# Sparse attention and a feed-forward layer on one core: decoding the weights by a parametric Relu, and batch 1 in two rounds of visits

## The chip, the cores and the metric

The kernel runs on one core of a Trainium2 chip. The core has TensorE (matrix products into PSUM; PE in the profile, PEld its weight loads), VectorE (DVE), ScalarE (ACT), GpSimd (POOL) and the DMA queues that SyncE (SP) starts. The metric is the device time of one execution in microseconds; lower is better.

## The reference, cut to what matters

Eight batches, eight heads, 576 tokens, 64 columns per head. Scores below the row's maximum less tau are dropped; the attention output of all heads is one row of 512 per token and goes through a feed-forward layer with weights of 512 x 2048 and 2048 x 512.

```python
scores = scale * np.matmul(q, k.transpose(0, 1, 3, 2))
thresh = np.max(scores, axis=-1, keepdims=True) - tau
scores = np.where(scores >= thresh, scores, -1000000000.0)
scores = scores - np.max(scores, axis=-1, keepdims=True)
attn = np.exp(scores)
attn = attn / (np.sum(attn, axis=-1, keepdims=True) + 1e-09)
attn_out = np.matmul(attn, v)
...
h = x @ w_in
g = h * (1.0 / (1.0 + np.exp(-h)))
return (g @ w_out).astype(np.float32)
```

q, k and v are float32; the weights are float64, and the kernel is handed their raw 64-bit words.

## The kernel before, in words

**Order of the work.** One Python loop runs over score tiles; a list `todo` hangs other steps on tile numbers. A tile is 128 query rows of one head against 576 keys (or 64 rows of two heads). `visits` lists pairs of heads: batch 0 is visited in two rounds, "low" (the first 256 query columns, four tiles a pair) and "high" (the other 320, five tiles), and every later batch in one ("all", nine tiles, query columns in two ranges of 288). The loop holds 12 empty steps between the rounds of batch 0 (tiles 16 to 27) and one ahead of batch 1, whose tiles are 49 to 84; batch 2 begins at 85. A scheduler orders the instructions of each engine at compile time from the order in which they are emitted, priorities (`pri`) and a model of their times; each engine then runs its list in order.

**A tile.** Two products of the query tile with the rounded keys and their remainder (L412); VectorE finds the maximum (L422); ScalarE takes exponentials (L432); VectorE masks and sums (L441); ScalarE normalises (L454). GpSimd makes two halves of 16 bits of the result (L465, L468, L471; for tiles below 36 ScalarE makes the first, L463). A DMA transpose brings them into `wT`, and AV (L496) multiplies them with the halves of V. The low round of batch 0 goes another way (`soft3_direct`, `av_direct`), without halves.

**Keys and queries.** `load_qk` loads K and Q of a head five tiles ahead, each twice (two halves of the partitions). `split_k` rounds K on ScalarE (L324) and takes the remainder on GpSimd (L326). `split_q` does the like for Q; for batch 1 and later on ScalarE (L315) and VectorE (L316).

**Weights.** Each of 32 tiles of 128 x 512 (16 of w_in, 16 of w_out) is loaded as pairs of 32-bit words. `decode_weights`: GpSimd scales the upper word, read as a float, by 2^-112 (L179); VectorE shifts it left by 3, which drops the sign (L183), and ORs in the lower word's top bits (L186); TensorE sums the magnitudes over the partitions with a matrix of ones, four matmuls a tile (L197), which bounds the maximum in every partition (L202); ScalarE takes the sign of the upper word (L204) and GpSimd multiplies by it (L205). Once all 16 tiles of a matrix are decoded, `pow2_scales` makes a power-of-two scale, and `split_weights` makes two 16-bit parts: ScalarE the first (L211), VectorE the second, the scaled weight less the first part (L212). `W_PLAN` hangs decoding of w_in on tiles 0 to 9 and its split on 10 to 12, decoding of w_out on tiles 9 to 21 and its split on 22 to 25.

**Feed-forward units.** When all heads of a column range are through AV, `moe_units` makes units: 16 h units (12 matmuls each, L539, then L547 to L555 on ScalarE and VectorE) and 16 o units (12 matmuls, L570). For batch 0 a range brings both kinds at once. From batch 1 on the o units of a range are held and paired with the h units of the next. The loop issues units by a credit that grows by `rate` a tile: 1.3 and 0.8 for the ranges of batch 0, then the units that are waiting, divided by the tiles until the next batch's range, times 0.95.

Of the kernel before, what the change touches and what calls it, by code (L numbers as in the profile page):

```python
# [40 lines left out]
PRI_AV = 1500  # L41

# [10 lines left out]
def attention_moe(  # L53
# [52 lines left out]
    def pow2_scales(mx, name, across=True):  # L106


        k = name[0]
        one = const.tile([P, 1], F32, name=f"{name}_one", tag=f"{k}_one")  # L110
        nc.vector.tensor_reduce(out=one, in_=mx, op=ALU.max, axis=AX.X)
        if across:


            diag = const.tile([P, P], BF16, name=f"{name}_diag", tag="diag")
            nc.scalar.activation(diag, ident, AF.Copy, scale=one)
            allp = bank([P, P], f"{name}_ps", 0 if turn[1] == 3 else None)
            nc.tensor.matmul(allp, ones, diag, start=True, stop=True)
            one = const.tile([P, 1], F32, name=f"{name}_all", tag=f"{k}_all")
            nc.vector.tensor_reduce(out=one, in_=allp, op=ALU.max, axis=AX.X)  # L120
        cl = const.tile([P, 1], F32, name=f"{name}_cl", tag=f"{k}_cl")
        nc.vector.tensor_scalar(
            out=cl, in0=one, scalar1=2.0**-20, scalar2=2.0**47, op0=ALU.max, op1=ALU.min
        )
        e2 = const.tile([P, 2], I32, name=f"{name}_e2", tag=f"{k}_e2")
        nc.vector.tensor_scalar(
            out=e2[:, 0:1], in0=cl.bitcast(I32), scalar1=EXPMASK, scalar2=None, op0=ALU.bitwise_and
        )
        nc.vector.tensor_scalar(
            out=e2[:, 1:2], in0=cl.bitcast(I32), scalar1=EXPMASK, scalar2=EXPMASK,  # L130
            op0=ALU.bitwise_and, op1=ALU.bitwise_xor,
        )
# [39 lines left out]
    def decode_weights(i):  # L172
# [6 lines left out]
        nc.gpsimd.tensor_scalar(  # L179
            out=w, in0=top.bitcast(F32), scalar1=2.0**-112, scalar2=1.0,  # L180
            op0=ALU.mult, op1=ALU.mult,
# [14 lines left out]
        for j in range(4):  # L196
            nc.tensor.matmul(  # L197
                wps[n], ones, upper[:, j * P : (j + 1) * P],
                start=(c == 0 and j == 0), stop=(c == 3 and j == 3),
            )  # L200
        if c == 3:
            nc.vector.tensor_reduce(out=wmx[:, n : n + 1], in_=wps[n], op=ALU.max, axis=AX.X)  # L202
        sg = stage.tile([P, 512], F16, tag="wsg", name=f"wsg_{i}", bufs=2)
        nc.scalar.activation(sg, top.bitcast(F32), AF.Sign)  # L204
        nc.gpsimd.tensor_tensor(out=w, in0=w, in1=sg, op=ALU.mult)  # L205

    def split_weights(i):
        w = wst[:, i + WSPARE, :]
        hi = w16[:, i, 0:512]
        sc = wsc["in" if i < 4 * NK else "out"][:, 0:1]  # L210
        nc.scalar.activation(hi, w, AF.Copy, scale=sc)  # L211
        nc.vector.scalar_tensor_tensor(  # L212
            out=w16[:, i, 512:1024], in0=w, scalar=sc, in1=hi, op0=ALU.mult, op1=ALU.subtract
        )
# [33 lines left out]
    def vscale(b):  # L248
        vsc[b] = pow2_scales(vmx[b], f"v{b}")
        if b == 0:  # L250
            nc.vector.tensor_scalar(
                out=xscale, in0=vsc[0][:, 0:1], scalar1=2.0**-12, scalar2=None, op0=ALU.mult
            )
# [32 lines left out]
    def load_qk(v, h):  # L286
        b, hh = divmod(h, H)
        qr = sb.tile([P, S], F32, tag="qraw", name=f"qraw_{v}_{h}", bufs=2)
        kr = sb.tile([P, S], F32, tag="kraw", name=f"kraw_{v}_{h}", bufs=2)
        for r in range(2):  # L290
            nc.sync.dma_start(out=kr[r * D : (r + 1) * D, :], in_=kT[b, hh])
            nc.sync.dma_start(out=qr[r * D : (r + 1) * D, :], in_=qT[b, hh])
        qkraw[h] = qr, kr
# [6 lines left out]
    def split_q(h, tiles):  # L300
        qr = qkraw[h][0]
        odd = h % 2
        c0, c1 = 0, S
        if len(tiles) < 4:
            c0, c1 = (0, 320) if odd else (256, S)
# [293 lines left out]
    def moe_units(b, c0, n):  # L599
        if b == 0:  # L600
            return h_units(b, c0, n) + o_units(b, c0, n)
# [11 lines left out]
    visits += [(b, p, "all") for b in range(1, B) for p in range(NPAIR)]  # L613
# [7 lines left out]
    for v, (b, p, kind) in enumerate(visits):  # L621
        if kind == "high" and p == 0:
            tiles.extend([None] * GAP)
            first_high = len(tiles)
        if b == 1 and p == 0:
            tiles.extend([None] * GAP1)
# [14 lines left out]
        if kind == "low":  # L641
# [7 lines left out]
        for h, use, tl, last in ((ha, u, ta, last_a), (ha + 1, use_b, tb + [4] * (4 in ta), last_b)):  # L649
            at(use - LOAD, lambda v=v, h=h: load_qk(v, h))  # L650
# [8 lines left out]
    for b in range(B):  # L659
        u = start[b, 0]  # L660
        for p in range(NPAIR):
# [4 lines left out]
            else:  # L666
                at(u + 9 * p - 40, lambda b=b, p=p: load_v(b, p))
                at(u + 9 * p - 34, lambda b=b, p=p: vmax(b, p))
                at(u + 9 * p + 4, lambda b=b, p=p: split_v(b, p))
# [11 lines left out]
    def scale_in():  # L681
        wsc["in"] = pow2_scales(wmx[:, 0:4], "i_w", across=False)

    def scale_out():
        wsc["out"] = pow2_scales(wmx[:, 4:8], "o_w", across=False)
# [129 lines left out]
```

## Time and profile before

| | us |
|---|---|
| three runs | 1252.15, 1245.27, 1250.52 |
| median | 1250.52 |
| the profiled execution | 1244.94 |
| its span, first to last instruction | 1243.2 |

One execution was profiled. Busy time is what an engine's instructions take; matmuls are pipelined and their ends are modelled, so a busy TensorE is not TensorE at its peak. PEclk is the granted share of TensorE's clock. A group's mean is over all instructions of one line and shape in the stretch that was asked for. What ended an idle time is inferred from semaphores.

### The profile page before, as it was taken

Reading aid. Unit: us, or ns where it says so; the run is one execution under the profiler, and the core shown is the slowest. Engines: PE = TensorE matmul, PEld = TensorE weight load, DVE = VectorE, ACT = ScalarE, POOL = GpSimd, SP = SyncE. Lnnn points to the kernel's source line nnn. Section 1 sums busy time; section 2 is a strip of 40 time slices with the busy share of each in tenths; the row PEclk is TensorE's granted clock in tenths of the full one; section 3 lists DMA queues with packets and bytes.
Section 4 is the critical chain, followed back from the end, with each engine's and each line's share of the span. In section 5 each row is a group of like instructions: output and inputs, shape, how many; then the busy total and the mean of one; then the engine's idle time right before and its main releaser. Section 6 shows DMA issues by size and latency. Waiting matters only on the chain.

```text
span 1243.2 us, 26997 instructions
## 1 busy us (share of the span) xinstructions
PE 1140.7 (92%) x9400; PEld 897.4 (72%) x9400; DVE 961.3 (77%) x2627; ACT 818.0 (66%) x1505; POOL 759.4 (61%) x952
## 2 busy tenths in 40 slices
PE   5674879899799989999999999999999999999998
PEld 3453657676577767777888877787777877777777
DVE  7999998978888888989888957988689848333230
ACT  5787777766777667777777747776577847433331
POOL 4568988577778768786878708773688538200000
PEclk8996889899899999999999999999999999999999
DMA  9457867678868868888778638783687436200000
GB/s 297 127 177 179 186 130 146 132 151 167 151 130 145 166 133 147 148 158 172 143 140 152 137 90 154 143 148 101 110 168 148 87 73 116 54 15 16 12 14 24
DMA packets 363480, 158.15 MB, mean 127 GB/s; under 512 B 329552, under 2 KB 338256, under 8 KB 363344
## 3 DMA queue, kind: packets, MB, share of 16 engines
q1 hardware_dynamic: 363344, 156.43, 61.9%
q8 instruction: 74, 1.21, 0.4%
q14 instruction: 62, 0.51, 0.1%
HBM read 66.72 MB, written 9.44 MB: 61 GB/s over the span
## 4 chain that ended last, share of the span: by engine, by line
PE 54%; DVE 25%; DMA 6%; ACT 6%; issue 5%; POOL 4%; SPq 0%; ACTq 0%; POOLq 0%; DVEq 0%
PE o L570 20%; PE h L539 19%; PE s L412 7%; PE a L496 7%; DVE w L441 6%; DVE sm L422 5%; DMA vraw<-in_vL 3%; DVE qstack L316 3%; ACT w L432 2%; DMA wT<-hl 2%; DVE wst L212 2%; DVE h L548 1%; DVE gbuf L555 1%; ACT w L454 1%; DVE wst L186 1%
## 5 line engine op out<-in xcount | busy, mean ns | idle before, releaser
L539 PE MATMUL h<-x,wst 128*128 128x288 f16 (+2 forms) x3072 | 430.8, 290 | 12.7 <-DVE gbuf L555 10.2
L570 PE MATMUL o<-gbuf,wst 128*128 128x288 f16 (+2 forms) x3072 | 420.6, 287 | 8.2 <-ACT wst L580 6.5
L539 PEld LDWEIGHTS <-wst 128*128 128x128 f16 x3072 | 294.6, 99 | 102.0 <-issue 22.0
L570 PEld LDWEIGHTS <-wst 128*128 128x128 f16 x3072 | 293.2, 98 | 90.5 <-issue 11.4
L468 POOL TENSOR_TENSOR hl<-w,hl 128x512 f16<-128x512 f32 x272 | 329.3, 1211 | 14.5 <-ACT hl L463 2.1
L465 POOL TENSOR_SCALAR hl<-w 128x576 f16<-128x576 f32 x264 | 180.6, 687 | 190.8 <-ACT w L454 128.3
L432 ACT ACTIVATE w<-s,sm 128x576 f32<-128x576 f32 x288 | 210.5, 738 | 83.5 <-DVE sm L422 30.6
L441 DVE SCALAR_TENSOR_TENSOR w<-s,sm,w 128x576 f32<-128x576 f32 x288 | 232.0, 812 | 32.5 <-ACT w L432 30.2
L454 ACT ACTIVATE w<-w,sm 128x576 f32<-128x576 f32 x288 | 217.6, 770 | 52.4 <-DVE sm L449 49.3
L422 DVE TENSOR_REDUCE sm<-s 128x1 f32<-128x576 f32 x288 | 215.0, 749 | 31.9 <-PE s L412 28.2
L548 DVE SCALAR_TENSOR_TENSOR h<-th,h 128x288 f32<-128x288 f32 (+2 forms) x256 | 116.2, 455 | 108.5 <-ACT th L547 106.4
L547 ACT ACTIVATE th<-h,msc 128x288 f32<-128x288 f32 (+2 forms) x256 | 126.2, 497 | 106.0 <-PE h L539 104.7
L412 PE MATMUL s<-khi,qstack 128*128 128x288 f32 x608 | 158.7, 343 | 19.0 <-DVE w L441 14.5
L554 ACT ACTIVATE gbuf<-h 128x288 f16<-128x288 f32 (+2 forms) x256 | 103.5, 407 | 81.3 <-DVE h L548 80.2
L555 DVE SCALAR_TENSOR_TENSOR gbuf<-h,gbuf 128x288 f16<-128x288 f32 (+2 forms) x256 | 114.9, 451 | 40.4 <-ACT gbuf L554 39.6
L496 PE MATMUL a<-wT,v 128*64 128x288 f16 (+1 forms) x1680 | 131.3, 298 | 13.5 <-DMA wT<-hl 13.3
L412 PE MATMUL s<-klo,qstack 128*128 128x288 f32 x608 | 132.6, 300 | 0.0
L326 POOL TENSOR_TENSOR klo<-kraw,khi 128x576 fp32r<-128x576 f32 x64 | 95.2, 1487 | 56.5 <-ACT khi L324 53.8
L412 PEld LDWEIGHTS s<-khi,qstack 128*128 128x128 f32 x608 | 97.9, 196 | 41.9 <-issue 22.9
L496 PEld LDWEIGHTS <-v 128*64 128x64 f16 x1680 | 94.5, 113 | 40.1 <-issue 30.3
L412 PEld LDWEIGHTS s<-klo,qstack 128*128 128x128 f32 x608 | 100.3, 194 | 0.3
L471 POOL TENSOR_TENSOR hl<-w,hl 128x64 f16<-128x64 f32 x272 | 100.2, 368 | 0.0
(84 smaller groups left out, 866.5 us busy)
## 6 DMA issues: line engine op xcount, KB each, us to landing
qraw<-in_qT SPq DMA_DIRECT2D x128, 144.0 KB, 3.0
kraw<-in_kT SPq DMA_DIRECT2D x128, 144.0 KB, 3.0
vraw<-in_vL SPq DMA_DIRECT2D x32, 320.0 KB, 3.7
wraw<-in_w_out SPq DMA_DIRECT2D x16, 512.0 KB, 3.8
out_t<-wst SPq DMA_DIRECT2D x56, 144.0 KB, 2.2
wT<-hl SPq DMA_TRANSPOSE x304, 3.4
gbuf<-in_w_in SPq DMA_DIRECT2D x8, 512.0 KB, 7.5
wraw<-in_w_in SPq DMA_DIRECT2D x8, 512.0 KB, 6.0
```

Of the source, the lines that this page charges most:

```text
L412: nc.tensor.matmul(s_ps[:, j, :HALF], lhs, kk[:, j * HALF : (j + 1) * HALF], start=(n == 0), stop=(n == len(seq) - 1),)
L422: nc.vector.tensor_reduce(out=negm, in_=s_ps[:, :, :HALF], op=ALU.max, axis=AX.XY, negate=True)
L432: nc.scalar.activation(wtile[t].rearrange("p (j c) -> p j c", j=2), sps[t][:, :, :HALF], AF.Exp, bias=small[t][:, 0:1],)
L441: nc.vector.scalar_tensor_tensor(out=w3, in0=s_ps[:, :, :HALF], scalar=sm[:, 1:2], in1=w3, op0=ALU.is_ge, op1=ALU.mult, accum_out=sm[:, 2:3],)
L454: nc.scalar.activation(w, w, AF.Copy, scale=r)
L465: nc.gpsimd.tensor_scalar(out=fl[:, 0:S], in0=w, scalar1=1.0, scalar2=1.0, op0=ALU.mult, op1=ALU.mult)
L468: nc.gpsimd.tensor_tensor(out=fl[:, 640:1152], in0=w[:, 0:512], in1=fl[:, 0:512], op=ALU.subtract)
L496: nc.tensor.matmul(a_ps[odd * D : (odd + 1) * D, :n], vt[:, lo_v, odd, kv, :], wT[v, b * H + 2 * p + odd][:, kw, c0 - base : c0 - base + n ...
L539: nc.tensor.matmul(ph[:, :n], wi(c, f, lo_w), x16[b, lo_x][:, c, c0 : c0 + n], start=(k == 0), stop=(k == 11),)
L548: nc.vector.scalar_tensor_tensor(out=ph[:, :n], in0=th[:, :n], scalar=1.0, in1=ph[:, :n], op0=ALU.add, op1=ALU.mult,)
L555: nc.vector.scalar_tensor_tensor(out=g[:, 1, :n], in0=ph[:, :n], scalar=2.0**-14, in1=g[:, 0, :n], op0=ALU.mult, op1=ALU.subtract,)
L570: nc.tensor.matmul(ps[:, :n], wo(f, d, lo_w), g[:, lo_g, :n], start=(f == 0 and k == 0), stop=(f == NF - 1 and k == 2),)
```

## The change

Weights: ScalarE's Prelu takes the place of GpSimd's scaling. A positive word is scaled by 2^-112, a negative one by 2^-112 times 2^32, so that the bit that the shift by 3 moves into the sign place is set; Sign and the multiplication by it go. As the weights now carry their sign, each part is multiplied with itself, so that the sums of squares stand on the diagonal; `pow2_scales` spreads the maximum over the partitions for the weights too, and halves the exponent of a sum of squares. In the split, GpSimd scales the weight in place, ScalarE casts the first part, and GpSimd takes the difference.

Batch 1: it is visited like batch 0, four low visits and then four high ones, all by the DMA-transposed way. Each head's keys are loaded and split in both rounds, its queries by column ranges. Its first range makes h and o units at once; the second (320 columns) is held and paired with batch 2. The V steps of batch 1 get other tile numbers, and the bank of its V scale is fixed.

```diff
+HALVED = (1,)
...
-    def pow2_scales(mx, name, across=True):
+    def pow2_scales(mx, name, own=None, squared=False):
...
         nc.vector.tensor_reduce(out=one, in_=mx, op=ALU.max, axis=AX.X)
-        if across:
...
+        diag = const.tile([P, P], BF16, name=f"{name}_diag", tag="diag")
+        nc.scalar.activation(diag, ident, AF.Copy, scale=one)
+        allp = bank([P, P], f"{name}_ps", own)
+        nc.tensor.matmul(allp, ones, diag, start=True, stop=True)
+        one = const.tile([P, 1], F32, name=f"{name}_all", tag=f"{k}_all")
+        nc.vector.tensor_reduce(out=one, in_=allp, op=ALU.max, axis=AX.X)
         cl = const.tile([P, 1], F32, name=f"{name}_cl", tag=f"{k}_cl")
+        low, high = (2.0**-40, 2.0**94) if squared else (2.0**-20, 2.0**47)
...
+        if squared:
+            twice = const.tile([P, 1], F32, name=f"{name}_twice", tag=f"{k}_twice")
+            nc.vector.tensor_scalar(
+                out=twice, in0=cl, scalar1=2.0, scalar2=None, op0=ALU.mult
+            )
+            half = const.tile([P, 1], I32, name=f"{name}_half", tag=f"{k}_half")
+            nc.vector.tensor_scalar(
+                out=half, in0=twice.bitcast(I32), scalar1=1, scalar2=EXPMASK,
+                op0=ALU.logical_shift_right, op1=ALU.bitwise_and,
+            )
+            cl = const.tile([P, 1], F32, name=f"{name}_root", tag=f"{k}_root")
+            nc.vector.tensor_scalar(
+                out=cl, in0=half.bitcast(F32), scalar1=2.0**64, scalar2=None, op0=ALU.mult
+            )
...
-        nc.gpsimd.tensor_scalar(
-            out=w, in0=top.bitcast(F32), scalar1=2.0**-112, scalar2=1.0,
-            op0=ALU.mult, op1=ALU.mult,
+        nc.scalar.activation(
+            w, top.bitcast(F32), AF.Prelu, scale=2.0**-112, alpha=2.0**32
         )
...
+            part = upper[:, j * P : (j + 1) * P]
             nc.tensor.matmul(
-                wps[n], ones, upper[:, j * P : (j + 1) * P],
+                wps[n], part, part,
                 start=(c == 0 and j == 0), stop=(c == 3 and j == 3),
             )
...
-        sg = stage.tile([P, 512], F16, tag="wsg", name=f"wsg_{i}", bufs=2)
-        nc.scalar.activation(sg, top.bitcast(F32), AF.Sign)
-        nc.gpsimd.tensor_tensor(out=w, in0=w, in1=sg, op=ALU.mult)
...
-        nc.scalar.activation(hi, w, AF.Copy, scale=sc)
-        nc.vector.scalar_tensor_tensor(
-            out=w16[:, i, 512:1024], in0=w, scalar=sc, in1=hi, op0=ALU.mult, op1=ALU.subtract
+        nc.gpsimd.tensor_scalar(
+            out=w, in0=w, scalar1=sc, scalar2=1.0, op0=ALU.mult, op1=ALU.mult
+        )
+        nc.scalar.activation(hi, w, AF.Copy)
+        nc.gpsimd.tensor_tensor(
+            out=w16[:, i, 512:1024], in0=w, in1=hi, op=ALU.subtract
         )
...
-        vsc[b] = pow2_scales(vmx[b], f"v{b}")
+        vsc[b] = pow2_scales(vmx[b], f"v{b}", (None, 2)[b] if b < 2 else 0)
...
+    def qcols(h, tiles):
+        if len(tiles) > 3:
+            return 0, S
+        if 0 in tiles:
+            return (320, S) if h % 2 else (0, 256)
+        return (0, 320) if h % 2 else (256, S)
+
-    def load_qk(v, h):
+    def load_qk(v, h, tiles):
         b, hh = divmod(h, H)
+        c0, c1 = qcols(h, tiles)
...
             nc.sync.dma_start(out=kr[r * D : (r + 1) * D, :], in_=kT[b, hh])
-            nc.sync.dma_start(out=qr[r * D : (r + 1) * D, :], in_=qT[b, hh])
+            nc.sync.dma_start(out=qr[r * D : (r + 1) * D, c0:c1], in_=qT[b, hh, :, c0:c1])
...
-        if b == 0:
+        if b == 0 or (b == 1 and c0 == 0 and 1 in HALVED):
             return h_units(b, c0, n) + o_units(b, c0, n)
...
-    visits += [(b, p, "all") for b in range(1, B) for p in range(NPAIR)]
+    for b in range(1, B):
+        for kind in ("low", "high") if b in HALVED else ("all",):
+            visits += [(b, p, kind) for p in range(NPAIR)]
...
-                at(u + 9 * p - 40, lambda b=b, p=p: load_v(b, p))
-                at(u + 9 * p - 34, lambda b=b, p=p: vmax(b, p))
-                at(u + 9 * p + 4, lambda b=b, p=p: split_v(b, p))
+                pace, first = (4, 24) if b in HALVED else (9, 40)
+                at(u + pace * p - first, lambda b=b, p=p: load_v(b, p))
+                at(u + pace * p - first + 6, lambda b=b, p=p: vmax(b, p))
+                at(u + pace * p + pace // 2, lambda b=b, p=p: split_v(b, p))
...
-        wsc["in"] = pow2_scales(wmx[:, 0:4], "i_w", across=False)
+        wsc["in"] = pow2_scales(wmx[:, 0:4], "i_w", squared=True)
...
-        wsc["out"] = pow2_scales(wmx[:, 4:8], "o_w", across=False)
+        wsc["out"] = pow2_scales(wmx[:, 4:8], "o_w", 2, squared=True)
```

## Rows read from the trace of the kernel before

**Rows 1.** The page: busy us per engine, and busy tenths in 40 slices.
```profile
PE 1140.7 (92%) x9400; PEld 897.4 (72%) x9400; DVE 961.3 (77%) x2627; ACT 818.0 (66%) x1505; POOL 759.4 (61%) x952
...
PE   5674879899799989999999999999999999999998
DVE  7999998978888888989888957988689848333230
```

**Rows 2.** Windows: stretch, length, busy us (instructions) per engine, granted clock, DMA share, GB/s.
```profile
0.00:62.00 62.00, 36.30 (x189) 23.73 (x189) 52.04 (x130) 41.48 (x76) 31.65 (x38) 0.92 0.68 212
62.00:124.00 62.00, 37.71 (x233) 27.13 (x233) 60.78 (x131) 50.23 (x95) 45.76 (x42) 0.82 0.66 179
124.00:186.00 62.00, 48.13 (x367) 37.48 (x365) 60.26 (x145) 46.92 (x88) 55.73 (x60) 0.86 0.72 158
186.00:248.00 62.00, 56.14 (x451) 45.10 (x450) 56.91 (x156) 45.18 (x80) 42.90 (x54) 0.94 0.71 139
248.00:310.00 62.00, 57.71 (x461) 43.65 (x458) 50.86 (x146) 40.21 (x68) 48.11 (x63) 0.97 0.79 159
310.00:372.00 62.00, 51.05 (x403) 40.08 (x402) 53.23 (x160) 47.22 (x85) 46.13 (x60) 0.92 0.77 141
372.00:1085.00 713.00, 698.99 (x6047) 556.93 (x6045) 585.81 (x1674) 498.26 (x912) 489.08 (x638) 1.00 0.70 132
1085.00:1243.00 158.00, 154.73 (x1264) 123.34 (x1261) 41.37 (x90) 48.54 (x106) 0.00 (x0) 1.00 0.05 16
```

**Rows 3.** Groups, whole span: line, engine, operation, out<-in, shapes, count | busy us, mean ns | idle before.
```profile
L468 POOL TENSOR_TENSOR hl<-w,hl 128x512 f16<-128x512 f32 x272 | 329.3, 1211 | 14.5 <-ACT hl L463 2.1
...
L465 POOL TENSOR_SCALAR hl<-w 128x576 f16<-128x576 f32 x264 | 180.6, 687 | 190.8 <-ACT w L454 128.3 <-DVE h L548 35.7 <-DMA wT<-hl 21.2
...
L326 POOL TENSOR_TENSOR klo<-kraw,khi 128x576 fp32r<-128x576 f32 x64 | 95.2, 1487 | 56.5 <-ACT khi L324 53.8 <-PE s L412 2.7
...
L316 DVE SCALAR_TENSOR_TENSOR qstack<-qraw,gate,qstack 64x576 fp32r<-64x576 f32 x56 | 73.6, 1315 | 5.3 <-ACT qstack L315 3.6
...
L324 ACT ACTIVATE khi<-kraw 128x576 fp32r<-128x576 f32 x64 | 43.6, 681 | 7.9 <-PE s L412 7.0 <-DMA kraw<-in_kT 0.7
...
L204 ACT ACTIVATE wsg<-wraw 128x512 f16<-128x512 f32 x24 | 15.9, 667 | 7.4 <-DMA wraw<-in_w_out 6.3 <-POOL wst L205 1.1
...
L116 ACT ACTIVATE v_diag<-ident,v_one 128x128 bf16<-128x128 f32 x8 | 3.2, 396 | 1.2 <-DVE v_one L111 1.2
...
L120 DVE TENSOR_REDUCE v_all<-v_ps 128x1 f32<-128x128 f32 x8 | 2.2, 281 | 0.0
...
L349 ACT ACT_TABLE_LOAD x1 | 1.3, 1283 | 4.5 <-DMA gbuf<-in_qT 4.5
```

**Rows 4.** Groups of VectorE, then of GpSimd, from 62 to 186 us.
```profile
L212 DVE SCALAR_TENSOR_TENSOR wst<-wst,i_w_sc 128x512 f16<-128x512 f32 x16 | 17.8, 1109 | 0.0
...
L183 DVE TENSOR_SCALAR wst<-wst 128x512 int32<-128x512 int32 x18 | 17.6, 979 | 1.5 <-POOL wst L179 1.5
...
L212 DVE SCALAR_TENSOR_TENSOR wst<-wst,o_w_sc 128x512 f16<-128x512 f32 x13 | 12.2, 949 | 0.0
...
L468 POOL TENSOR_TENSOR hl<-w,hl 128x512 f16<-128x512 f32 x19 | 24.8, 1306 | 2.5 <-ACT hl L463 2.1
...
L205 POOL TENSOR_TENSOR wst<-wst,wsg 128x512 f32<-128x512 f32 x18 | 23.0, 1281 | 7.9 <-PE wps L197 4.2 <-DVE wst L183 1.7 <-ACT wT L368 1.5
...
L179 POOL TENSOR_SCALAR wst<-wraw 128x512 f32<-128x512 f32 x18 | 15.1, 840 | 5.6 <-DMA wraw<-in_w_out 4.7 <-DMA wraw<-in_w_in 0.5 <-DVE w L441 0.2
```

**Rows 5.** VectorE's timeline, two instructions of one line: start us, length us.
```profile
62.84 1.62 DVE L183 TENSOR_SCALAR wst<-wst 128x512 int32<-128x512 int32 x1 [1.10 <-POOL wst L179]
...
83.00 0.41 DVE L183 TENSOR_SCALAR wst<-wst 128x512 int32<-128x512 int32 x1
```

**Rows 6.** TensorE's timeline: the first matmuls of 288 columns at L539.
```profile
303.66 1.27 PE L539 MATMUL h<-x,wst 128*128 128x288 f16 x9
```

**Rows 7.** Groups of VectorE from 186 to 312 us.
```profile
L441 DVE SCALAR_TENSOR_TENSOR w<-s,sm,w 128x576 f32<-128x576 f32 x37 | 29.7, 810 | 2.9 <-ACT w L432 2.5
```

More of the change, by code (lines that the diff above doesn't have):

```diff
@@ L111, in pow2_scales @@
         nc.vector.tensor_reduce(out=one, in_=mx, op=ALU.max, axis=AX.X)
-        if across:
[L115 to L120, printed above, removed]
+        diag = const.tile([P, P], BF16, name=f"{name}_diag", tag="diag")
[4 more added lines that the diff above has]
+        nc.vector.tensor_reduce(out=one, in_=allp, op=ALU.max, axis=AX.X)
         cl = const.tile([P, 1], F32, name=f"{name}_cl", tag=f"{k}_cl")
+        low, high = (2.0**-40, 2.0**94) if squared else (2.0**-20, 2.0**47)
         nc.vector.tensor_scalar(
-            out=cl, in0=one, scalar1=2.0**-20, scalar2=2.0**47, op0=ALU.max, op1=ALU.min
+            out=cl, in0=one, scalar1=low, scalar2=high, op0=ALU.max, op1=ALU.min
         )
+        if squared:
[12 more added lines that the diff above has]
+            )
         e2 = const.tile([P, 2], I32, name=f"{name}_e2", tag=f"{k}_e2")
@@ L302, in split_q @@
         odd = h % 2
-        c0, c1 = 0, S
-        if len(tiles) < 4:
-            c0, c1 = (0, 320) if odd else (256, S)
+        c0, c1 = qcols(h, tiles)
         src = qr[:, c0:c1]
@@ L621, in attention_moe @@
     for v, (b, p, kind) in enumerate(visits):
-        if kind == "high" and p == 0:
+        if b == 0 and kind == "high" and p == 0:
             tiles.extend([None] * GAP)
             first_high = len(tiles)
-        if b == 1 and p == 0:
+        if b == 1 and p == 0 and kind != "high":
             tiles.extend([None] * GAP1)
@@ L640, in attention_moe @@
         use_b = last_a if 4 in ta else last_a + 1
-        if kind == "low":
+        if b == 0 and kind == "low":
             at(u - LOAD, lambda v=v: load_direct(v))
@@ L649, in attention_moe @@
         for h, use, tl, last in ((ha, u, ta, last_a), (ha + 1, use_b, tb + [4] * (4 in ta), last_b)):
-            at(use - LOAD, lambda v=v, h=h: load_qk(v, h))
+            at(use - LOAD, lambda v=v, h=h, tl=sorted(tl): load_qk(v, h, tl))
             at(use - 3, lambda h=h: split_k(h))
```

## The prediction

> **What bounds the kernel now.** I read the page's busy shares first, then the windows, then the groups of instructions of single stretches, and last a few single instructions. [rows 1] The tensor engine is busy for 92% of the span and the vector engine for 77%, but the two rows in slices show that these averages hide two regimes: the tensor engine's digits are 4 to 8 for the first quarter and 9 almost everywhere behind it, while the vector engine is at 7 to 9 from the start. [rows 2] The windows put numbers on it. From 372 us to 1085 us the tensor engine is busy 699.0 of 713 us at a granted clock of 1.00, and from 1085 us on it works alone, 154.7 of 158 us. Nothing but less tensor work, or work started sooner, moves those 871 us. All that can be won lies ahead of 372 us. There the tensor engine is idle for 25.7, 24.3 and 13.9 us in the first three windows, and for 5.9, 4.3 and 11.0 us in the next three.
>
> So there are two places. The prologue (0 to 186 us) decodes and splits the weights, and from 62 us the vector engine is busy 60.8 and 60.3 of 62 us: it is the bound there. The second place is 186 to 372 us, batch 1's attention and the start of batch 2's. No engine is full there; the tensor engine misses 21.2 us, and its clock stands at 0.94, 0.97 and 0.92. Taking the missing clock as lost work adds 56.1 x 0.06 + 57.7 x 0.03 + 51.1 x 0.08 = 9.2 us, so at most 30 us can be had in it.
>
> **Weights: what is removed, added and moved.** Per weight tile (32 of them) the decode loses a GpSimd multiplication of the raw words and a GpSimd multiplication by the sign. [rows 4] These take 0.840 and 1.281 us, about 68 us in all. Sign on ScalarE goes too, 0.667 us [rows 3], and Prelu comes in its place with the same shape and input. The trace shows no Prelu: it may cost as little as Sign with its 0.667 us, and I take that, or bring table loads (a rival below). The four weight matmuls stay in number and shape; only their stationary operand changes. In the split, VectorE loses its subtraction: 17.8 us for the 16 tiles of w_in and 12.2 us for 13 of w_out between 62 and 186 us [rows 4], 30.0 us of the 121.0 us that it is busy there. GpSimd gains two operations per tile. The multiplication is nearest to L465 (0.687 us for 576 columns against 512) and the subtraction has the operands of L468 (1.211 us) [rows 3]: 1.90 us per tile, 61 us in all. It could be as high as 1.306 us for the subtraction, which L468 takes in this stretch [rows 4], and then the 32 cost 64 us.
>
> The point is where that lands. Over the whole run GpSimd's account is even, 68 against 61 us. But decoding starts at the first load, and splitting only once a whole matrix is decoded. In 62 to 186 us GpSimd is busy 45.8 + 55.7 = 101.5 us [rows 2]. It loses 23.0 + 15.1 = 38.1 us [rows 4] and gains 29 x 1.90 = 55 us if the same 29 splits fall there, 61 us if all do: 118 to 124 of 124 us. VectorE falls to 91 us. The stretch changes its bound from VectorE at 121 us to GpSimd at 118 to 124 us, so the 30 us that VectorE gives back are mostly not a gain.
>
> One thing in the stretch's favour is left. L183, one plain shift on VectorE, takes 0.41 us in one place and 1.62 us in another [rows 5], and 0.979 us on average [rows 4]; the long ones lie beside GpSimd's work. While w_in is decoded GpSimd is now almost idle. Fourteen of the 32 shifts lie ahead of 62 us, and 14 x (0.979 - 0.41) = 8 us is the most that they can give; I take 5 us.
>
> The Trainium skill's "GPSIMD Engine Reference" (section "Engine selection") speaks against this change: it advises VectorE for elementwise work, as GpSimd is about twice as slow with two inputs. The rows agree only in part: VectorE's subtraction takes 1.109 and 0.949 us here, GpSimd's like it 1.211. By the page's ratio the subtractions would cost 32 x 2 x 1.03 = 66 us instead of 39, and the stretch would grow by 27 us; an estimate that I don't follow, as L468 is the same operation on the engine itself. The same page (section "Key points") says that the two engines contend for their SBUF interfaces, which is what the two shifts show.
>
> The scale chain grows: both matrices now spread their maximum over the partitions, a diagonal copy of 0.396 us and a reduction of 0.281 us [rows 3] with a small matmul between, and three more tiny operations of at most 0.281 us each: about 1.3 us ahead of the first split, on the path for w_in; for w_out it hides behind the high tiles' softmax. Two waits change engine. Prelu waits for the weights' transfer where the GpSimd multiplication did; behind it in ScalarE's queue stand exponentials and normalisations, and VectorE's masking (L441) waits for those. Sign waited for the same transfer in the same queue, so this adds nothing that the rows don't hold already. GpSimd's split waits for the scale; behind it stand the halves of the softmax weights (L465, L468), then the DMA transposes, then AV: a late scale now delays batch 0's second round, where before it delayed VectorE's subtraction. Prologue: -5 + 1.3, say **-4 us**, from -20 us (splits start early and GpSimd overlaps well) to +10 us (GpSimd at 124 us, stretched by 8% as 1.306 to 1.211).
>
> **Batch 1 in two rounds.** Its 36 score tiles stay 36, and scores, AV and the feed-forward have the same columns. Eight heads are prepared twice: 8 more K loads (two transfers each, on SP's queue; SP's other work there is loads and transposes, and the new transfers stand between them), 8 more K roundings of 0.681 us on ScalarE, 8 more K remainders of 1.487 us on GpSimd = 11.9 us [rows 3]. Query halves add instructions, not columns: from the L316 row (1.315 us for 576 columns) two halves cost between 1.3 and 2.6 us, I take 1.6, so 2 us more on VectorE. GpSimd is busy 42.9 + 48.1 = 91.0 us in 186 to 310 us [rows 2], so 103 of 124 us: this hides behind the softmax chain. Without that cover it would cost 12 us. The V steps of batch 1 move too: its four loads go from tiles 9 to 36 to tiles 25 to 37, their reductions 6 tiles behind, and the splits to tiles 51 to 63 from 53 to 80. They are the same instructions and transfers, still ahead of the first AV, so I cost the move at nothing; a load that came late would hold the reduction, the V scale and all four splits behind it.
>
> What is gained is early feed-forward work. The first unit of batch 1 starts at 303.66 us [rows 6]. By the code it becomes available at tile 69 instead of 89. VectorE passes 37 tiles in the 126 us from 186 us on [rows 7], 3.4 us each, so 20 tiles are 68 us: the first unit could start near 236 us. By the loop's credits, 0.8 units per tile until tile 69 and then (18.4 + 32) / 20 x 0.95 = 2.4, some 93 units are issued by tile 89 where there were 62. A unit is 12 matmuls of 1.27 / 9 = 0.141 us [rows 6], 1.7 us, so 31 units are 52 us of tensor work, more than the 30 us of gaps. Gaps ahead of 248 us can't be reached (5.9 us, 3.4 us of clock); behind it 4.3 + 11.0 us idle and 5.8 us of clock, 21 us, can. VectorE is the next limit: 56.9 + 50.9 us of 124 us [rows 2], and 16 more hidden units finish in it. I take **-12 us**, from 0 to -25 us.
>
> **The sum.** The profiled execution took 1244.9 us with a span of 1243.2 us. 1244.9 - 4 - 12 = 1229 us. The runs shown have a median of 1250.5 us, 5.6 us above it; from there the same sum gives 1234.5 us. I forecast between them, 1232 us.
>
> **Rivals.** *Given back in batch 2.* By tile 125 old and new loops have issued the same 110 to 112 units, so what batch 1 gets early, batch 2 lacks: 0.5 units per tile instead of 1.4, 31 x 1.7 = 52 us less, where 372 us on is full now. Backlog (what the tensor engine couldn't do in batch 1) and a faster attention speak against a full loss. If the 12 us are lost again, 1241 us by the profile and 1246.5 us by the median: within 0.5%, which is about what a measurement of this kernel can tell from no change.
>
> *GpSimd becomes the bound.* In 62 to 186 us its 124 us stretch to 134, the transposed weights come late, AV and with it the first half of batch 1 move back by 10 us, and 11.9 us of K remainders follow on the same engine, so that the second term shrinks to nothing. Result 1255 us by the profile, 1260 us by the median. It decides if GpSimd is over 95% busy there and batch 1 starts over 5 us later. For it: 118 to 124 us. Against it: GpSimd's slack behind 186 us.
>
> *VectorE's relief comes through.* Were the high round's softmax paced by VectorE alone, 20 us would come off the prologue and 15 to 20 us behind it: about 1210 us. GpSimd's 118 us speak against it.
>
> *Table loads.* The run has a single ACT_TABLE_LOAD of 1.283 us [rows 3] for Exp, Tanh, Copy and Sign together. If Prelu asked for another table, 32 of them between exponentials would cost up to 64 x 1.283 = 82 us; ScalarE is busy 138.6 of 186 us in the prologue [rows 2], so 35 us would show, 1280 us or more. The Trainium skill's "ScalarE: Activation LUTs" (section "Table sets: the hidden batching unit") has loads at each change of set, but says that cheap functions stand in every set; no run so far shows it for Prelu.
>
> **Chances and range.** My sum 0.52, relief in full 0.10, given back 0.20, GpSimd 0.14, table loads 0.04. Faster by over 0.5% (below 1244.3): 0.52 + 0.10 and a fifth of the given-back case, 0.66. Within 0.5%: 0.16. Slower: 0.18. The forecast's own range is 1216 to 1243 us; with the others, 1206 to 1258 us leaves out the table loads, about half of the GpSimd case and a part of the full relief.
>
> **What would show it.** Right: GpSimd over 110 us and VectorE under 105 us of 62 to 186 us; L183 near 0.6 us in the decode of w_in; batch 1's first unit before 250 us; the window 310 to 372 us with the tensor engine over 57 us; still one table load. Wrong: batch 1's scores starting over 5 us later, tensor gaps of over 8 us per 62 us between 372 and 500 us, or a prologue shorter by over 12 us.

## The result and the profile after

The changed kernel takes 1253.43 us (median of 20 runs, 1249.41 to 1259.94), the kernel before 1247.99 us (20 runs, 1244.11 to 1252.15). The ratio is 1.005, 95% interval 1.0037 to 1.0064: slower by 0.5%, where 1.5% less was forecast. Its profiled execution has a span of 1250.5 us. The windows of the kernel after, with the columns of [rows 2]:

```profile
0.00:62.00 62.00, 39.16 (x217) 25.43 (x217) 49.24 (x138) 46.66 (x87) 4.84 (x11) 0.94 0.75 227
62.00:124.00 62.00, 47.75 (x298) 35.94 (x297) 55.97 (x151) 53.87 (x103) 54.20 (x56) 0.81 0.84 211
124.00:186.00 62.00, 38.22 (x285) 28.51 (x285) 49.96 (x128) 40.11 (x79) 59.59 (x70) 0.88 0.51 107
186.00:248.00 62.00, 50.77 (x399) 38.97 (x400) 42.92 (x121) 41.68 (x73) 58.21 (x70) 0.82 0.84 160
248.00:310.00 62.00, 60.45 (x467) 44.43 (x466) 55.72 (x159) 47.80 (x87) 54.77 (x70) 1.00 0.85 162
310.00:372.00 62.00, 55.28 (x482) 45.81 (x481) 56.82 (x164) 47.01 (x88) 37.76 (x49) 1.00 0.63 134
372.00:434.00 62.00, 59.02 (x509) 46.45 (x507) 50.28 (x151) 42.68 (x79) 48.48 (x66) 0.97 0.82 154
434.00:496.00 62.00, 54.81 (x445) 41.15 (x444) 55.29 (x147) 45.41 (x82) 46.58 (x59) 0.94 0.74 150
```

and the two windows of the kernel before that were not shown:

```profile
372.00:434.00 62.00, 61.41 (x539) 48.40 (x537) 55.00 (x155) 45.98 (x83) 50.79 (x66) 1.00 0.86 155
434.00:496.00 62.00, 58.45 (x495) 45.71 (x494) 53.62 (x156) 44.35 (x81) 46.07 (x60) 1.00 0.77 140
```

GpSimd is busy 4.8 us in the first window where it was 31.7, and 54.2, 59.6 and 58.2 of 62 us in the next three; VectorE, the bound before, falls to 50.0 and 42.9 us in the last two of them. TensorE runs ahead at first (47.8 against 37.7 us from 62 to 124 us) and loses it: 38.2 and 50.8 us against 48.1 and 56.1, the second at a clock of 0.82. It then fills 248 to 372 us better than before, and less well from 372 to 496 us: 59.0 and 54.8 us against 61.4 and 58.5. Groups of the kernel after, GpSimd's from 62 to 186 us, then VectorE's shift (L195, 0 to 62 us), its OR (L198, 62 to 186 us), then ScalarE's Prelu and table load (0 to 62 us):

```profile
L225 POOL TENSOR_TENSOR wst<-wst 128x512 f16<-128x512 f32 x24 | 28.9, 1214 | 0.1
L221 POOL TENSOR_SCALAR wst<-wst,i_w_sc 128x512 f32<-128x512 f32 x16 | 12.7, 815 | 1.3 <-DVE msc L270 1.3
L221 POOL TENSOR_SCALAR wst<-wst,o_w_sc 128x512 f32<-128x512 f32 x16 | 12.1, 775 | 0.0
...
L195 DVE TENSOR_SCALAR wst<-wst 128x512 int32<-128x512 int32 x16 | 6.8, 428 | 0.8 <-ACT wst L192 0.7
...
L198 DVE SCALAR_TENSOR_TENSOR wst<-wraw,wst 128x512 int32<-128x512 int32 x16 | 17.4, 1084 | 0.0
...
L192 ACT ACTIVATE wst<-gbuf 128x512 f32<-128x512 f32 x8 | 5.4, 674 | 6.3 <-DMA gbuf<-in_w_in 6.3
...
L368 ACT ACT_TABLE_LOAD x1 | 1.3, 1283 | 4.4 <-DMA gbuf<-in_qT 4.4
```

The split's two instructions cost 0.815 and 0.775, and 1.214 us, close to the 1.90 us a tile of the forecast. Prelu takes 0.674 us, and there is one table load. The shift is down to 0.428 us beside an idle GpSimd (0.979 in [rows 4]). Beside a full one VectorE's OR takes 1.084 us. Three V splits (L290) take 0.88, 1.24 and 5.92 us there. The long V split, three places of GpSimd's and TensorE's timelines, and two of TensorE's waits from 144 to 248 us (who waits <- for whom: us, times, longest); then one place and one such wait of the kernel before:

```profile
169.99 5.92 DVE L290 SCALAR_TENSOR_TENSOR v<-vraw,v_sc,v 128x640 f16<-128x640 f32 x1
...
144.52 11.40 POOL L221 TENSOR_SCALAR wst<-wst,o_w_sc 128x512 f32<-128x512 f32 x15
...
214.98 1.15 POOL L225 TENSOR_TENSOR wst<-wst 128x512 f16<-128x512 f32 x1
...
320.99 0.82 PE L558 MATMUL h<-x,wst 128*128 128x256 f16 x6
...
PE s L431 <- DVE w L460: 18.4, 8, 6.2
...
PE o L589 <- POOL wst L225: 1.0, 2, 0.6
```

```profile
321.02 0.54 PE L539 MATMUL h<-x,wst 128*128 128x288 f16 x3
...
PE s L412 <- DVE w L441: 1.2, 3, 0.6
```

GpSimd scales fifteen tiles of w_out in one block, but takes most of their differences one or two at a time between the softmax halves; the last ends at 216 us. Batch 0's o units (L589) need them. TensorE's direct wait for these parts is only 1.0 us. It waits 18.4 us ahead of score tiles for a mask (L460), against 1.2 us before; that it stands there because the o units can't be run in between is argued here, and tested by `w_out_pool` below. Batch 0's units end late, at 321 us instead of 304, and batch 1's first (L558, 256 columns) starts at 320.99 us, where the kernel before had it at 303.66 us [rows 6] and I expected 236 us. The 17 us between the two are less than they look: the kernel before runs nine of that unit's 12 matmuls at 303.66 us, and the three that are left not before 321.02 us, behind the last pair's AV.

### The profile page after: what moved, and what is told of

It reads as the page before. It is cut to its first block, busy times and chain, and to the rows that moved or that the text cites. A ratio compares the mean times of both kernels' runs of the same rounds, so it can differ in the third digit from the quotient of the medians.

```text
span 1250.5 us, 27033 instructions
## 1 busy us (share of the span) xinstructions
PE 1147.4 (92%) x9402; PEld 896.7 (72%) x9402; DVE 933.4 (75%) x2611; ACT 822.8 (66%) x1523; POOL 758.1 (61%) x960
## 4 chain that ended last, share of the span: by engine, by line
PE 58%; DVE 15%; DMA 7%; ACT 7%; POOL 7%; issue 5%; SPq 1%; ACTq 0%; POOLq 0%; DVEq 0%
PE o L589 23%; PE h L558 19%; PE s L431 8%; PE a L515 6%; DVE w L460 5%; DMA wT<-hl 3%; DVE sm L441 3%; DVE qstack L335 2%; ACT w L451 2%; POOL hl L487 2%; ACT w L473 2%; DMA vraw<-in_vL 1%; POOL wst L225 1%; POOL hl L484 1%; DMA wraw<-in_w_out 1%
## 5 line engine op out<-in xcount | busy, mean ns | idle before, releaser
L558 PE MATMUL h<-x,wst 128*128 128x288 f16 (+2 forms) x3072 | 429.6, 290 | 9.9 <-DVE gbuf L574 9.4
L589 PE MATMUL o<-gbuf,wst 128*128 128x288 f16 (+2 forms) x3072 | 426.4, 289 | 7.0 <-ACT wst L599 4.3
L558 PEld LDWEIGHTS <-wst 128*128 128x128 f16 x3072 | 294.7, 99 | 98.4 <-issue 17.6
L589 PEld LDWEIGHTS <-wst 128*128 128x128 f16 x3072 | 293.8, 99 | 93.6 <-issue 12.0
L484 POOL TENSOR_SCALAR hl<-w 128x576 f16<-128x576 f32 x264 | 177.6, 675 | 173.3 <-ACT w L473 98.9
L460 DVE SCALAR_TENSOR_TENSOR w<-s,sm,w 128x576 f32<-128x576 f32 x288 | 233.1, 813 | 60.5 <-ACT w L451 57.8
L473 ACT ACTIVATE w<-w,sm 128x576 f32<-128x576 f32 x288 | 219.7, 772 | 51.5 <-DVE sm L468 48.8
L345 POOL TENSOR_TENSOR klo<-kraw,khi 128x576 fp32r<-128x576 f32 x72 | 106.5, 1479 | 97.7 <-ACT khi L343 88.3
L515 PE MATMUL a<-wT,v 128*64 128x288 f16 (+2 forms) x1680 | 128.8, 293 | 4.9 <-DMA wT<-hl 4.9
L515 PEld LDWEIGHTS <-v 128*64 128x64 f16 x1680 | 89.9, 110 | 33.2 <-issue 19.5
L490 POOL TENSOR_TENSOR hl<-w,hl 128x64 f16<-128x64 f32 x272 | 96.9, 356 | 0.0
```

The lines of the kernel that those rows point to most:

```text
L460: nc.vector.scalar_tensor_tensor(out=w3, in0=s_ps[:, :, :HALF], scalar=sm[:, 1:2], in1=w3, op0=ALU.is_ge, op1=ALU.mult, accum_out=sm[:, 2:3],)
L473: nc.scalar.activation(w, w, AF.Copy, scale=r)
L484: nc.gpsimd.tensor_scalar(out=fl[:, 0:S], in0=w, scalar1=1.0, scalar2=1.0, op0=ALU.mult, op1=ALU.mult)
L515: nc.tensor.matmul(a_ps[odd * D : (odd + 1) * D, :n], vt[:, lo_v, odd, kv, :], wT[v, b * H + 2 * p + odd][:, kw, c0 - base : c0 - base + n ...
L558: nc.tensor.matmul(ph[:, :n], wi(c, f, lo_w), x16[b, lo_x][:, c, c0 : c0 + n], start=(k == 0), stop=(k == 11),)
L589: nc.tensor.matmul(ps[:, :n], wo(f, d, lo_w), g[:, lo_g, :n], start=(f == 0 and k == 0), stop=(f == NF - 1 and k == 2),)
```

## The experiments

Each kernel was timed against the kernel before; ratios are to it. Theory A puts the loss on GpSimd's split of the weights, theory B on the two rounds; the other letters are explained in the expectations.

**The two halves of the change.** `weights_only` sets `HALVED = ()` in the changed kernel. `halves_only` is the kernel before with the two rounds, so it has the decode, the split and the scale of before. The edit of the first:

```diff
-HALVED = (1,)
+HALVED = ()
```

> The changed weights (Prelu decode, split by GpSimd) alone; batch 1 in one round as before. Theory A (GpSimd is the bound from 93 to 217 us, the split of w_out ends late, batch 0's o units wait for it, and the two rounds of batch 1 win back part of that): slower than before by 6 to 15 us, ratio 1.005 to 1.012, GpSimd over 115 of 124 us in 93 to 217 us. Theory B (the weights are about even, and the two rounds lose what they gain because batch 2 runs short of units): between 4 us faster and 3 us slower, ratio 0.997 to 1.002.

> Batch 1 in two rounds alone; the weights are decoded and split as before. Theory A: faster than before by 4 to 12 us, ratio 0.990 to 0.997, with the window 310 to 372 us over 57 us of tensor time. Theory B: slower by 2 to 8 us, ratio 1.002 to 1.006, with gaps of 8 us and more per 62 us in batch 2.

Measured (ratios to the runs of before on the same chip): weights alone 1246.5 us, 0.9999 [0.9984, 1.0015]; two rounds alone 1248.9 us, 1.001 [0.9992, 1.0028]. Neither is told from no change, and B is the nearer theory: with the changed weights the two rounds cost 6 us (ratio 1.005 against 0.9999), with the old ones 2 us, which the interval doesn't tell from nothing. But an even sum can have two large terms, so the split was undone by itself.

**The split back on VectorE**, with two rounds and with one:

```diff
-        nc.gpsimd.tensor_scalar(
-            out=w, in0=w, scalar1=sc, scalar2=1.0, op0=ALU.mult, op1=ALU.mult
-        )
-        nc.scalar.activation(hi, w, AF.Copy)
-        nc.gpsimd.tensor_tensor(
-            out=w16[:, i, 512:1024], in0=w, in1=hi, op=ALU.subtract
-        )
+        nc.scalar.activation(hi, w, AF.Copy, scale=sc)
+        nc.vector.scalar_tensor_tensor(
+            out=w16[:, i, 512:1024], in0=w, scalar=sc, in1=hi, op0=ALU.mult, op1=ALU.subtract
+        )
```

> The changed kernel with one part undone: the split is ScalarE's scaled copy and VectorE's one subtraction again; Prelu decode and two rounds stay. GpSimd has some 60 us less to do, VectorE 30 us more. Theory A: faster than before by 10 to 20 us, ratio 0.984 to 0.992, and the last split of w_out 10 us or more ahead of where the changed kernel has it (216 us). Theory B: within 5 us of the changed kernel, ratio to before 1.001 to 1.009.

> Prelu decode alone: the split on VectorE as before, batch 1 in one round. Theory A: faster than before by 3 to 12 us, ratio 0.990 to 0.998, as GpSimd loses 68 us and VectorE's shifts shorten. Theory B: about even with before, ratio 0.997 to 1.002, and faster than the same kernel with two rounds.

Measured: 1231.2 us with two rounds, 0.9874 [0.9853, 0.9894], and 1224.1 us with one, 0.9814 [0.9795, 0.9834], which is below the range of either theory. Prelu decode alone wins 23 us; GpSimd's split gives 22 of them back (1246.5 - 1224.1); two rounds cost 7 us here. Theory A holds for the weights in kind, though it put the gain too low; B holds for the rounds. The kernel with 1224.1 us (Prelu decode, both splits on VectorE, batch 1 in one round) is called the one-round kernel from here on.

**Which split.** `w_in_pool` and `w_out_pool` start from the one-round kernel and give one matrix to GpSimd (the test below, or its opposite, ahead of the change's three instructions):

```diff
+        if i >= 4 * NK:
...
+            return
```

> Prelu decode, batch 1 in one round; w_in is split by GpSimd as in the change, w_out by VectorE as before. Both on VectorE take 1224.1 us, both on GpSimd 1246.5 us. Theory A1 (it is w_out's split, queued among the softmax halves of batch 0's second round, that holds the o units): 1222 to 1230 us. Theory A2 (GpSimd's load as such, alike for both): 1232 to 1238 us.

> Prelu decode, batch 1 in one round; w_out is split by GpSimd as in the change, w_in by VectorE as before. Theory A1: 1238 to 1247 us, nearly all of the 22 us. Theory A2: 1232 to 1238 us.

Measured: 1230.0 us, 0.9876 [0.9851, 0.9901], and 1240.4 us, 0.9955 [0.9935, 0.9976]: 6 and 16 us of the 22. A1 has both in its ranges, the first at their edge; so w_out's split is most of it, and w_in's is not free. A window of `w_out_pool`, then windows of the one-round kernel (the later three are for the rounds):

```profile
186.00:248.00 62.00, 48.06 (x349) 36.20 (x347) 47.29 (x113) 39.00 (x65) 56.06 (x69) 0.83 0.71 135
```

```profile
186.00:248.00 62.00, 58.23 (x493) 46.51 (x492) 52.78 (x150) 43.56 (x77) 50.83 (x66) 0.97 0.77 143
248.00:310.00 62.00, 59.89 (x486) 45.73 (x486) 51.35 (x146) 41.34 (x71) 45.32 (x59) 0.97 0.80 151
310.00:372.00 62.00, 56.57 (x484) 44.53 (x483) 57.25 (x175) 50.51 (x97) 49.63 (x66) 1.00 0.85 150
372.00:434.00 62.00, 60.36 (x529) 48.75 (x528) 54.15 (x155) 43.28 (x79) 45.38 (x59) 1.00 0.80 155
```

From 186 us TensorE has 48.1 us of work at a clock of 0.83 in the one and 58.2 us at 0.97 in the other, with GpSimd at 56.1 and 50.8 us.

**Where the 23 us come from.** `busy_pool` is the one-round kernel with GpSimd's two former instructions a tile put back on a scratch tile:

```diff
...
+        nc.gpsimd.tensor_scalar(
+            out=scr[0], in0=scr[0], scalar1=1.0, scalar2=1.0, op0=ALU.mult, op1=ALU.mult
+        )
+        nc.gpsimd.tensor_tensor(out=scr[0], in0=scr[0], in1=scr[0], op=ALU.mult)
```

> The split on VectorE, Prelu decode, batch 1 in one round, and per decoded tile two GpSimd instructions on a scratch tile that nobody reads, of the sizes of the two that the change took away (a scaling and a product, some 1.9 us a tile, 60 us in all). Theory C (the gain of the Prelu decode is GpSimd's time and the VectorE instructions that it stretches): most of the 23 us is lost again, 1238 to 1248 us, and VectorE's shift is back near 0.9 us. Theory D (the gain is the shorter chain of one decoded tile, load to shift): 1224 to 1230 us.

Measured: 1239.4 us, 0.9946 [0.993, 0.9962]: 15 of the 23 us are lost to instructions whose results nothing reads. Groups up to 186 us, the shift in this kernel and in the one without them:

```profile
L196 DVE TENSOR_SCALAR wst<-wst 128x512 int32<-128x512 int32 x32 | 22.0, 691 | 2.7 <-ACT wst L193 2.6
```

```profile
L195 DVE TENSOR_SCALAR wst<-wst 128x512 int32<-128x512 int32 x32 | 15.8, 496 | 3.9 <-ACT wst L192 3.8
```

Theory C carries some two thirds, and its time is in C's range: 32 shifts take 6.2 us more, though 0.691 us each is short of the 0.9 that C wanted. The other third may be the chain, as D has it; the run does not separate that. Nor is the copy exact: waiting for no transfer, these instructions come early, and GpSimd is busy 51.5 us of the first 62 us where it was 31.7 before.

**Why two rounds cost.**

```diff
-HALVED = (1,)
+HALVED = (1, 2)
```

> The split on VectorE, Prelu decode, and batches 1 and 2 both in two rounds. Theory G (what two rounds start early in batch 1 is missing in batch 2; the gap only moves): batch 2's units come 20 tiles sooner, the gap at 372 to 434 us closes; 1222 to 1228 us, ahead of the 1231.2 us with batch 1 alone in two rounds. Theory K (the second preparation of the keys slows the attention): another 4 to 8 us lost, 1235 to 1239 us. Theory R (2.4 units per tile put their ScalarE and VectorE steps ahead of the softmax): 1231 to 1240 us.

`spread` leaves batch 1's own second range out when the rate is worked out:

```diff
-            nxt = [r[0] for r in ready if r[0] > t + 1]
+            nxt = [r[0] for r in ready if r[0] > t + 1 and (b != 1 or r[1] != 1)]
```

> The split on VectorE, Prelu decode, batch 1 in two rounds, and the loop's rate for batch 1's units worked out to batch 2's first range (0.85 to 1.3 units per tile instead of 2.4 and then 0.5). Theory R: 1222 to 1227 us, as with one round. Theory G: the gap in batch 2 closes but batch 1's gaps come back, 1224 to 1231 us. Theory K: no change, 1230 to 1233 us.

`k_twice` repeats both instructions of `split_k` for batch 1, `k_twice5` for batch 5:

```diff
+        for _ in range(2 if h // H == 1 else 1):
```

> The split on VectorE, Prelu decode, batch 1 in one round, but each of its eight heads rounds its keys twice on ScalarE and takes the remainder twice on GpSimd (5.4 and 11.9 us more work; no further loads). Theory K: 4 to 8 us slower than the 1224.1 us without, 1228 to 1232 us. Theories G and R: within 2 us of it.

> As k_twice, but the doubled preparation of the keys is that of batch 5, where the tensor engine has work in store. Theory K: no loss there, 1222 to 1228 us; the 15 us of k_twice are then the price of delaying batch 1's attention. Theory N (any edit gives the scheduler another order, and that alone moves the time by some 10 us): 1230 to 1240 us here too.

`no_second_k` loads no keys in batch 1's second round (its scores there are of other keys), and `split_k` returns:

```diff
...
+        if kr is None:
+            khl[h] = khl[2 * H - 2 + h % 2]
+            return
```

> The split on VectorE, Prelu decode, batch 1 in two rounds, but in batch 1's second round no keys are loaded or prepared: all four visits use the keys of the last pair of the first round (so batch 1's scores in that round are of other keys). Theory K: the two rounds then gain, 1215 to 1224 us. Theory G: the shortage of units in batch 2 stays, 1227 to 1232 us, near the 1231.2 us with the keys prepared again.

Measured: `halved12` 1233.3 us, 0.9895 [0.9874, 0.9917]; `spread` 1230.6 us, 0.9873 [0.9848, 0.9898]; `k_twice` 1239.2 us, 0.9947 [0.9929, 0.9964]; `k_twice5` 1223.8 us, 0.9814 [0.9789, 0.984]; `no_second_k` 1244.8 us, 0.9976 [0.9953, 0.9999]. The totals fit no theory throughout. `halved12` is in R's range alone; `spread` is outside R's, inside K's and just inside G's; `k_twice` and `no_second_k` are outside all of them; `k_twice5` is in K's range, and N missed. So I looked at where each kernel's matmuls lie. Windows of `split_dve`, then two rows of its matmuls with the weights alone (the units, and the 128 of the decode that both kernels have), and such rows of the one-round kernel:

```profile
248.00:310.00 62.00, 60.70 (x506) 47.11 (x505) 51.05 (x146) 44.22 (x77) 51.82 (x66) 1.00 0.90 168
310.00:372.00 62.00, 54.77 (x486) 46.55 (x486) 54.40 (x164) 43.98 (x82) 44.23 (x58) 0.97 0.79 148
372.00:434.00 62.00, 53.90 (x435) 40.41 (x434) 57.39 (x160) 47.01 (x87) 44.94 (x57) 0.94 0.78 157
...
0.00:372.00 372.00, 171.19 (x1277) 0.92 0.78 174
372.00:434.00 62.00, 31.48 (x210) 0.94 0.78 157
```

```profile
0.00:372.00 372.00, 166.84 (x1214) 0.91 0.77 169
372.00:434.00 62.00, 43.97 (x336) 1.00 0.80 155
```

Two rounds run 63 more of these matmuls by 372 us, and 126 fewer in the next 62 us: what was early is given back twice. All of TensorE's matmuls, up to 496 us and from 496 to 1060 us, in the one-round kernel, `split_dve`, `halved12`, `spread`, `no_second_k` and `k_twice`:

```profile
0.00:496.00 496.00, 422.95 (x3308) 324.15 (x3309) 438.27 (x1234) 375.92 (x684) 313.24 (x395) 0.93 0.77 164
496.00:1060.00 564.00, 556.62 (x4793) 442.54 (x4792) 455.18 (x1308) 390.10 (x716) 379.13 (x494) 1.00 0.68 129
...
0.00:496.00 496.00, 417.87 (x3234) 318.84 (x3235) 441.69 (x1225) 378.17 (x690) 324.76 (x400) 0.93 0.78 168
496.00:1060.00 564.00, 556.57 (x4817) 444.54 (x4816) 457.29 (x1318) 392.69 (x719) 380.33 (x497) 1.00 0.68 131
...
0.00:496.00 496.00, 418.62 (x3261) 320.37 (x3262) 437.44 (x1213) 377.52 (x699) 314.69 (x385) 0.94 0.77 167
...
0.00:496.00 496.00, 422.41 (x3274) 321.59 (x3275) 445.14 (x1236) 379.88 (x694) 327.12 (x402) 0.94 0.79 169
496.00:1060.00 564.00, 551.84 (x4740) 439.02 (x4738) 459.48 (x1307) 389.51 (x713) 379.90 (x494) 1.00 0.68 129
...
0.00:496.00 496.00, 415.64 (x3221) 316.70 (x3222) 443.90 (x1212) 370.52 (x674) 304.40 (x383) 0.93 0.74 161
496.00:1060.00 564.00, 550.98 (x4690) 436.44 (x4689) 462.34 (x1317) 393.09 (x717) 381.67 (x499) 0.99 0.67 130
...
0.00:496.00 496.00, 426.36 (x3235) 323.40 (x3236) 433.69 (x1211) 375.25 (x679) 319.57 (x395) 0.92 0.75 162
496.00:1060.00 564.00, 549.69 (x4706) 437.14 (x4705) 463.95 (x1318) 392.90 (x717) 382.13 (x500) 0.99 0.69 131
```

By 496 us `split_dve` has started 74 matmuls fewer than the one-round kernel, 9 us at the 0.12 us that a matmul takes on average, and none fewer behind it: so the 7 us lie ahead of 496 us. `halved12` makes good 27 of the 74 and `spread` 40, so both the units missing in batch 2 (G) and the rate (R) seem to have a part, and neither is the whole; both lose more behind 496 us than they won (the profiled execution of `spread` took 1234.3 us, 4 us over its median, so its loss there is uncertain). `no_second_k` makes good none, which speaks against the keys (K), although keys prepared twice in one round, `k_twice`, cost 73.

Behind 496 us `no_second_k` and `k_twice` start 127 and 87 matmuls fewer than the kernels they were made from, 15 and 10 us, although no instruction of batches 3 to 7 was edited. TensorE's compiled order of these batches is another: counted in the traces, ahead of the nineteenth score tile of batch 7 stand 4333 matmuls of units in the one-round kernel, 4264 in `split_dve`, and 4283 in both of these. That the order makes the loss is likely, not shown. N, which `k_twice5` spoke against, is then there after all, but not at every edit, and the totals of these runs can't be set to one theory's account. TensorE's timeline in `split_dve`, then in the one-round kernel:

```profile
237.57 1.17 PE L512 MATMUL a<-wT,v 128*64 128x256 f16 x18
...
297.09 1.58 PE L555 MATMUL h<-x,wst 128*128 128x256 f16 x13
...
422.24 1.91 PE L512 MATMUL a<-wT,v 128*64 128x288 f16 x28
...
428.60 0.82 PE L428 MATMUL s<-khi,qstack 128*128 128x288 f32 x2 [4.46 <-DVE w L457]
...
431.54 3.99 PE L555 MATMUL h<-x,wst 128*128 128x288 f16 x24
```

```profile
301.34 0.29 PE L555 MATMUL h<-x,wst 128*128 128x288 f16 x1
```

Batch 1's first unit starts at 297.09 and at 301.34 us, 4 us apart. In `split_dve` the last product that it needs, the AV of its range, ends at 238.7 us; TensorE's list holds batch 0's units until 297 us. From 248 to 372 us TensorE is busy 115.5 us with two rounds and 116.5 with one: no gap was filled. From 424.1 to 428.6 us TensorE has nothing but the next score tile, for which it waits; batch 2's first unit comes at 431.54 us.

**The store queue.** GpSimd's timeline in `split_dve` shows one more wait, for a transpose; theory S is that it stands in SP's queue behind stores of batch 1's early o units:

```profile
359.08 0.67 POOL L481 TENSOR_SCALAR hl<-w 128x576 f16<-128x576 f32 x1 [7.81 <-DMA wT<-hl]
```

Three kernels issue the output stores from ScalarE's queue:

```diff
-            nc.sync.dma_start(out=outT[d * P : (d + 1) * P, c : c + n], in_=o[:, :n])
+            nc.scalar.dma_start(out=outT[d * P : (d + 1) * P, c : c + n], in_=o[:, :n])
```

> split_dve (split on VectorE, Prelu decode, batch 1 in two rounds) with the output stores issued from ScalarE's queue instead of SP's. Theory S (batch 1's early o units put stores into SP's in-order queue ahead of batch 2's transposes, and these wait for the units): the 7.8 us wait of GpSimd at 359 us is gone, batch 2's attention ends 8 us sooner, 1222 to 1227 us. Theory G (the shortage of units in batch 2 does not depend on that): 1229 to 1233 us, as split_dve.

> The same stores from ScalarE's queue with batch 1 in one round, as a control. Theories S and G: within 3 us of the 1224.1 us with SP's queue.

> Two rounds without the second load and preparation of the keys (batch 1's second round uses other keys), and the stores from ScalarE's queue. Theories K and S together: two rounds cost nothing any more, 1218 to 1225 us. Theory G: 1229 us or more; if the loss lies behind 496 us again, the order of the late batches, in which this kernel and k_twice are alike, makes it, and none of the three.

Measured: 1228.7 us, 0.9846 [0.9827, 0.9864]; 1226.7 us, 0.9837 [0.9814, 0.9859]; 1233.7 us, 0.9874 [0.9851, 0.9897]. A window of `stores_act`, then its longest single GpSimd wait from 186 to 440 us (who waits <- for whom: us, times, longest):

```profile
372.00:434.00 62.00, 54.10 (x449) 39.82 (x448) 59.73 (x165) 48.22 (x91) 46.22 (x59) 1.00 0.82 154
```

```profile
POOL hl L481 <- ACT khi L340: 11.4, 1, 11.4
```

GpSimd's wait for the transposes falls from 7.8 to 2.2 us, one of 11.4 us for the keys' rounding has come, and the gap from 372 us stays (54.1 us). Batch 2's last score tile, the 108th, is masked 1 us sooner (406.4 us against 407.4), where S had 8. S is not borne out; it may be worth the 2 us. `stores_act_no_second_k` is the cleaner test of K: from 496 us on it starts 4813 matmuls, `stores_act` 4826, and yet it is not faster with the second preparation left out (5 us slower, with intervals that overlap). So K is not what two rounds cost.

What all seven two-round kernels with the split on VectorE share (`halves_only` too) is the gap: 53.1 to 56.8 us from 372 to 434 us, where all kernels with one round have 59.1 to 61.4. Where two rounds lose is shown, and that the early units are missed there. Why more units (`halved12`) fill only a part of the gap stays open.

The fastest kernel is the one with Prelu decode alone: 1224.1 us, faster than both (`k_twice5`, the same with work done twice, is level with it).

## Why the prediction was wrong

*The weights, forecast -4 us, measured -0.4 us (`weights_only`).* The total was near by luck: two terms, both mis-sized, cancelled. I wrote that the stretch from 62 us changes its bound from VectorE's 121 us to GpSimd's 118 to 124 us; the trace has GpSimd at 113.8 us of 124, and at 121 us from 93 to 217 us. That step was right in kind, though VectorE fell only to 106 us, not to 91. The first mis-sized term is what the decode gives back when GpSimd is free: I took 5 us, at most 8, for VectorE's shortened shifts; Prelu alone is worth 23 us. I had counted only one instruction's length, not the work that queues behind GpSimd and VectorE there; GpSimd's two old instructions put back cost 15 of the 23 us. The second is GpSimd's split: I set it even against the 30 us that VectorE gives back, and it costs 22 us net, 16 of them with w_out.

*GpSimd's rival* had the right engine and the wrong path, and its 1255 us are near the total for another reason. I expected AV and batch 1's attention to slip; batch 0's last score tile, the 36th, is masked at 169.5 us against 183.0 before, and its last AV starts at 191.2 against 194.4. What slips are w_out's parts (the last at 216 us) and with them the o units of batch 0's first range, which end at 238.7 us where they ended at 209.2.

*Two rounds, forecast -12 us, measured +2 to +7.* The failing step is "the first unit could start near 236 us". I took the tile at which a unit becomes available for the time at which TensorE gets to it, and never asked when batch 0's units end: at 303.8 us before, 297 to 321 us here. My own count said as much: 18.4 units of batch 0 are still waiting at tile 69, so by the loop's credits batch 1's first is issued at tile 77, and not at 69; in one round it is issued at 92. These 15 tiles came to 4 us on TensorE (`split_dve`). Gaps could be filled only behind that, from 310 us, and these were 11 us of idle time before and 5 us once the decode is faster. Against that stands the rival *given back in batch 2*: issued early, batch 1's units run out ahead of batch 2's. I gave it 0.20 and priced it at all of the gain; it took more, as 63 matmuls won by 372 us were followed by 126 lost by 434 us. Batch 2's attention itself is not late at its end: its last tile is masked at 407.4 us in `split_dve` and at 406.6 in the one-round kernel.

*Table loads* did not occur. *VectorE's relief* did not come through: VectorE is busy 15 us less from 62 to 186 us, and TensorE does no more there (86.0 us against 85.8). The GPSIMD Engine Reference of the Trainium skill (section "Key points", contention with VectorE) is borne out beyond my use of it: 0.496 us for the shift in the one-round kernel, against 0.691 with the two GpSimd instructions put back (`busy_pool`). Its ratio of two would have made the subtraction dearer than the 1.214 us that the trace shows.

## What to carry to other kernels

Before work is released earlier, look at what stands ahead of it in the list of the engine that is to run it: a unit whose inputs are there at 239 us starts at 297 us behind a list that is full until then. An account that is even over the whole run says nothing where one matrix must wait for all of itself; weigh an engine's load in the stretch where the work lands. Undo the parts of a change one by one even if its sum is nil: here -23 and +22 us lay under it.

## What was not expected of the hardware

One VectorE instruction took seven times as long as its like: a split of V, 128 x 640, took 5.92 us in the changed kernel, with six GpSimd instructions in a row beside it. Others of that kernel beside a busy GpSimd took 0.88 and 0.87 us (at 147 and 197 us), and the mean over the span of the kernel before is 0.945 us; so a busy GpSimd alone doesn't make such a stretch, and what does is not shown. And an edit in one batch moved matmul counts by up to 127 in a window of 564 us some batches later, likely through the compiled order, which is as much as most effects that were looked for.
